# Moving the 28th row of a weight tile onto eight DMA engines in a decode kernel, with two rows added on VectorE

## The chip, the cores and the metric

The kernel runs on one core of one Trainium2 chip. The metric is device time in microseconds (us), measured over repeated executions. "Span" is the time from the first to the last recorded instruction of the core; the difference "time minus span" is what a run costs around that.

The profile names the engines PE (TensorE matmul), PEld (its weight load), DVE (VectorE), ACT (ScalarE), POOL (GpSimd) and SP (SyncE, which here only issues loads). The core has 16 DMA engines, which this document numbers 0 to 15.

## The reference, cut to what matters

One token: attention over a long cache, plus a small MLP, summed into one row of 1,024 numbers.

```python
x = A_x                                  # [1, 1, 1024] bf16
xn = _layernorm(x, axis=-1)
return x + _A_ref(xn, k_cache, v_cache, wq, wo) + _B_ref(xn, w1, w2, w3, w4)

# _A_ref: q = x @ wq (32 heads of 128); softmax(q k^T / sqrt(128)) v over 65,536 keys
#         and 4 kv heads; then @ wo
# _B_ref: ... gelu(layernorm(x1) @ w3) @ w4 ...      w4 is [3584, 1024]
```

Weights and caches are 169.87 MB of bf16 and each byte is used once, so the kernel is a stream of loads with arithmetic hidden under it.

## The kernel before

The loads go one after another through one queue into three slots of 8 MB. The last two are V of the last unit and w4. In w4's slot each of the 128 partitions holds 28 rows of 1,024 numbers (2 KB each); they come in pieces of 8, 12, 5, 2 and 1 rows per partition, so that TensorE can work on a piece while the next ones arrive. The code calls row c of all partitions together column c of w4.

```python
W4_PIECES = (8, 12, 5, 2, 1)
FIRST = 3;  AT_ONCE = 1;  NARROW = 8;  AHEAD = 5
...
elif it == "w4":
    w4_v = B_w4.rearrange("(m c) n -> m c n", c=FC)          # FC = 28
    c0 = 0
    for n in W4_PIECES:
        go(out=t[:, c0 * D:(c0 + n) * D], in_=w4_v[:, c0:c0 + n, :].rearrange("p c n -> p (c n)"))
        c0 += n
```

Everything is summed in one PSUM tile psB (two halves of 512). The x row enters by two float32 matmuls early, the wo rows of three head groups by two float32 matmuls at 384 us. The tail (the last NARROW = 8 of the 28 columns of w4) goes by matmuls of 256 columns to two other PSUM tiles, which four float32 matmuls join with psB:

```python
copy_projection()                    # wo rows of three groups: PSUM -> SBUF
summed = compute_v(NU - 1)
with tc.issue_after(summed):
    add_projection()                 # 2 float32 matmuls into psB
compute_w4(0, FIRST)                 # columns 0..2 of w4
with tc.issue_after(tail["gathered"]):       # "gathered": the matmul pm_e of the last group
    compute_w4(FIRST, early)         # columns 3..7
projected = project(HKV - 1)
with tc.issue_after(projected):
    compute_w4(early, FC - NARROW)   # columns 8..19: the 12-row piece, 24 matmuls
nc.scalar.copy(out=sums[:], in_=psB[0:64, :])
...
narrow_rows(FC - NARROW, FC - NARROW + AHEAD, start=True)     # the 5-row piece, 20 matmuls
quarter_acc(lambda j: ident_f[...], lambda j, h: sums[:, 256 * h:256 * (h + 1)])   # psB joins
narrow_rows(FC - NARROW + AHEAD, FC)                          # the 2- and 1-row pieces, 12 matmuls
nc.scalar.copy(out=out_t[:, 0, :], in_=quarters[0][0:64, 0:256])
nc.vector.tensor_copy(out=out_t[:, 1, :], in_=quarters[1][64:128, 0:256])   # the last cast
nc.scalar.dma_start(out=..., in_=out_t[31:33]...)
```

## Time and profile before

| | before |
|---|---|
| time, median of 3 (range) | 400.86 us (400.77 to 400.88) |
| profiled run: time, span, mean granted clock | 400.66, 398.7, 0.812 |
| last landing of the 12-row piece | 391.50 us |
| last landing of w4 (one-row piece) | 396.50 us |
| start of the last VectorE cast | 396.90 us |

The page of the kernel before, parts 2 and 3: the busy tenths of the DMA engines in 40 slices of the span, then each queue with its packets, megabytes and share of the 16 engines' time.

```profile
DMA  9998999999999999999999999999999998999996
q1 hardware_dynamic: 4128, 169.87, 98.9%
q8 instruction: 9, 0.15, 0.2%
q14 instruction: 1, 0.01, 0.0%
```

The load queue keeps the engines busy for 98.9% of the span, so nothing under it is worth anything by itself. Queue 8 moves nine blocks of instructions.

The chain of waits of the kernel before, its end (start us, us, what):

```profile
363.39 33.10 DMA big<-in_B_w_dram
396.50 0.04 issue
396.54 0.34 PE pm_r L504 x4
396.88 0.02 issue
396.90 0.43 DVE out_t L521
```

The run ends with w4's loads; only four matmuls and a cast stand between the last landing and the store.

The timeline of PE in the kernel before, from 384 us (start us, us, engine, line, operation, operands, count, and in brackets the idle time before it and its releaser):

```profile
385.02 0.82 PE L225 MATMUL psB<-big,hT 128*32 128x512 bf16 x6
386.76 0.49 PE L438 MATMUL pm_e<-ol,sel8big 128*128 128x129 f32 x2 [0.92 <-DVE ol L437]
387.18 1.25 PE L225 MATMUL psB<-big,hT 128*32 128x512 bf16 x10
388.33 1.90 PE L225 MATMUL psB<-big,oT 128*32 128x512 bf16 x16
391.54 2.77 PE L225 MATMUL psB<-big,hT 128*32 128x512 bf16 x24 [1.31 <-DMA big<-in_B_w_dram]
...
396.54 0.29 PE L504 MATMUL pm_r<-big,hT 128*32 128x256 bf16 x4 [0.24 <-DMA big<-in_B_w_dram]
```

TensorE waits 1.31 us for the 12-row piece and again 0.24 us for the last row: it has some slack at each piece. The last four matmuls start 0.04 us after the last landing, and the cast 0.40 us after it.

Each DMA engine adds one to a load's semaphore when its share has landed, and the trace records the time of each increment. This is the one-row piece of the kernel before, sorted (the trace doesn't say which engine is which):

```
394.61 394.62 394.65 394.76 394.84 394.94 394.98 | 395.76 | 396.08 396.23 396.28 396.30 396.31 396.33 396.45 396.50
```

Seven engines are done 1.5 to 1.9 us before the last eight, and one stands between. Early in the run all 16 are within 0.46 us. After each 16 KB block of instructions (queue 8, about 1.05 us each) one more engine stands about 1.5 us further back; after the one block of 8 KB (queue 14, 0.33 us, at 113.21) one engine goes from at most 0.42 to 1.19 us back. Eight of the nine 16 KB blocks are through by 384.1 us, and eight engines form the late group.

### The profile page before, as it was taken

How to read it: one execution, taken by the hardware profiler on the slowest of the kernel's cores; microseconds unless marked ns; L12 is line 12 of the kernel's file. 1: busy time of each engine (PE TensorE's matmuls, PEld its weight loads, DVE VectorE, ACT ScalarE, POOL GpSimd, SP SyncE). 2: the span in 40 equal slices, each digit the busy share in tenths (PEclk: the TensorE clock that was granted, in tenths of full speed). 3: DMA queues.
4: the chain of work that ended last, by engine and by line, in shares of the span. 5: the costliest groups of instructions: out<-in, count | busy, mean ns of one | idle time of the engine just before them, and what ended most of it. 6: DMA issues, size and time to landing. Idle time of an engine off the chain costs nothing.

```text
span 398.7 us, 2595 instructions
## 1 busy us (share of the span) xinstructions
PE 229.6 (58%) x1372; PEld 44.2 (11%) x878; DVE 209.4 (53%) x155; ACT 27.6 (7%) x36; POOL 5.3 (1%) x28
## 2 busy tenths in 40 slices
PE   0461960591569238733974296519462955394996
PEld 0210000010100010011001010200020101010132
DVE  0620010974296559633963795269439942894140
ACT  1001010003000200020002000200110001002000
POOL 2000000000000000000000000000000000000000
PEclk9995996596869787966695889679956896698799
DMA  9998999999999999999999999999999998999996
GB/s 421 421 443 377 444 434 487 441 421 421 416 422 434 421 480 442 421 421 427 422 434 427 447 460 427 416 427 427 441 429 427 454 441 385 418 460 429 409 432 254
DMA packets 4144, 170.03 MB, mean 427 GB/s; under 512 B 419, under 2 KB 421, under 8 KB 678
## 3 DMA queue, kind: packets, MB, share of 16 engines
q1 hardware_dynamic: 4128, 169.87, 98.9%
q8 instruction: 9, 0.15, 0.2%
q14 instruction: 1, 0.01, 0.0%
q10 hardware_dynamic: 6, 0.00, 0.0%
HBM read 169.87 MB, written 0.00 MB: 426 GB/s over the span
## 4 chain that ended last, share of the span: by engine, by line
DMA 56%; DVE 21%; PE 17%; ACT 2%; another core or an unknown queue 2%; issue 1%; SPq 0%; DVEq 0%; ACTq 0%
DMA big<-in_A_k_cache_dram 42%; DVE big L361 15%; PE sc L366 11%; DMA big<-in_B_w_dram 8%; DMA big<-in_A_wq_dram 5%; PE oacc L416 4%; DVE p_sb L387 2%; DVE mx L371 2%; ACT p_sb L384 2%; PE psq L291 1%; SPq L187 0%; PE pm_mx L373 0%; DVE m L375 0%; PE pm_mx L380 0%
## 5 line engine op out<-in xcount | busy, mean ns | idle before, releaser
L366 PE MATMUL sc<-big,qdiag 128*128 128x512 bf16 x512 | 129.3, 414 | 67.0 <-DVE big L361 61.4
L361 DVE STREAM_TRANSPOSE big<-big 128x4096 f32<-128x4096 f32 x32 | 139.4, 4413 | 50.3 <-DMA big<-in_A_k_cache_dram 50.3
L416 PE MATMUL oacc<-big,p_sb 128*32 128x512 bf16 x512 | 43.0, 502 | 34.5 <-DVE p_sb L387 34.5
L371 DVE TENSOR_REDUCE mx<-sc 128x1 f32<-128x2048 f32 x8 | 18.3, 2292 | 29.8 <-PE sc L366 29.8
L366 PEld LDWEIGHTS <-qdiag 128*128 128x128 bf16 x128 | 13.2, 103 | 178.7 <-issue 145.9
L384 ACT ACTIVATE p_sb<-sc,nball 128x2048 bf16<-128x2048 f32 x8 | 15.7, 1967 | 220.9 <-DVE nball L382 220.9
L387 DVE STREAM_TRANSPOSE p_sb<-p_sb 128x2048 bf16<-128x2048 bf16 x8 | 18.5, 2311 | 18.0 <-ACT p_sb L384 18.0
L416 PEld LDWEIGHTS <-p_sb 128*32 128x32 bf16 x512 | 16.1, 122 | 58.2 <-DVE p_sb L387 35.1
L291 PE MATMUL psh<-big,ln_rep_b 128*32 128x512 bf16 (+1 forms) x64 | 12.4, 943 | 8.8 <-DMA big<-in_B_w_dram 8.8
L456 PE MATMUL o_acc<-big,oT 128*1 128x512 bf16 x48 | 13.2, 445 | 2.4 <-ACT p_sb L384 2.4
L373 PE MATMUL pm_mx<-ident_f,mx 128*1 128x128 f32 x8 | 2.4, 296 | 19.1 <-DVE mx L371 19.1
L425 DVE SCALAR_TENSOR_TENSOR og<-oacc,wb,og 128x512 f32<-128x512 f32 x4 | 3.0, 751 | 18.4 <-PE oacc L416 18.4
L330 DVE STREAM_TRANSPOSE h_row<-h_row 128x896 bf16<-128x896 bf16 x1 | 1.1, 1111 | 22.0 <-ACT h_row L329 22.0
L239 PE MATMUL pm_ln<-ln_rowsum_a,ones_f 128*128 128x1 f32 x2 | 0.6, 348 | 12.8 <-DVE ln_rowsum_a L237 12.8
L438 PE MATMUL pm_e<-ol,sel8big 128*128 128x129 f32 x8 | 2.3, 370 | 8.8 <-DVE ol L437 8.8
L315 POOL COPY qdiag<-qx 32x32 bf16<-32x32 bf16 x16 | 3.2, 202 | 279.3 <-PE sc L366 250.9
L230 DVE STREAM_TRANSPOSE x_t<-x_row 32x256 bf16<-32x256 bf16 x4 | 2.5, 616 | 8.3 <-DMA x_row<-in_A_x_dram 8.3
L463 DVE COPY big<-o_acc 1x1024 f32<-1x1024 f32 x1 | 1.2, 1211 | 10.5 <-PE o_acc L456 10.5
L225 PE MATMUL psB<-big,hT 128*32 128x512 bf16 x40 | 4.8, 380 | 1.3 <-DMA big<-in_B_w_dram 1.3
L291 PE MATMUL psq<-big,ln_rep_a 128*32 128x512 bf16 x64 | 5.0, 482 | 0.9 <-DMA big<-in_A_wq_dram 0.9
L521 DVE CAST out_t<-pm_r 64x256 bf16<-64x256 f32 x1 | 0.4, 426 | 8.6 <-PE pm_r L504 8.6
L380 PE MATMUL pm_mx<-ident_f,rep 1*128 1x1 f32 x8 | 1.8, 229 | 5.0 <-DVE rep L377 5.0
(101 smaller groups left out, 76.2 us busy)
## 6 DMA issues: line engine op xcount, KB each, us to landing
big<-in_A_wo_dram SPq DMA_DIRECT2D x1, 8192.0 KB, 35.8
big<-in_B_w_dram SPq DMA_DIRECT2D x1, 7168.0 KB, 38.0
big<-in_B_w_dram SPq DMA_DIRECT2D x3, 2048.0 KB, 35.5
big<-in_B_w_dram SPq DMA_DIRECT2D x1, 3072.0 KB, 29.5
big<-in_B_w_dram SPq DMA_DIRECT2D x1, 1280.0 KB, 32.2
big<-in_B_w_dram SPq DMA_DIRECT2D x1, 512.0 KB
big<-in_B_w_dram SPq DMA_DIRECT2D x1, 256.0 KB, 33.1
big<-in_A_k_cache_dram SPq DMA_DIRECT2D x8, 42.3
```

Of the source, the lines that this page charges most:

```text
L225: return nc.tensor.matmul(psB[32 * j:32 * j + 32, :], lhsT=lhsT.to_broadcast([lhsT.shape[0], 32]), rhs=rhs, start=start, stop=False, tile_ ...
L230: nc.vector.transpose(out=x_t[32 * a:32 * a + 32].rearrange("p c j -> p (c j)"), in_=x_row[:, 256 * a:256 * (a + 1)].rearrange("p (i c) -> ...
L291: nc.tensor.matmul(acc[32 * q:32 * q + 32, i, 0:n], lhsT=rep[:, c, :], rhs=cols(c, i, q), start=(c == 0), stop=(c == DC - 1), tile_positio ...
L315: nc.gpsimd.tensor_copy(out=qdiag[at, LEAD:].rearrange("p (x c) -> p x c", x=4)[:, :, 32 * a:32 * a + 8], in_=qx[at, :, 8 * g:8 * g + 8])
L361: nc.vector.transpose(out=words, in_=words)
L366: nc.tensor.matmul(sc[:, e, :], lhsT=qdiag[:, c0:c0 + P], rhs=cols[:, s, e, :, b2, :, r], start=(s == 0 and b2 == 0 and r == 0), stop=(s = ...
L371: nc.vector.reduce_max(out=mx[:], in_=sc[:].rearrange("p e n -> p (e n)"), axis=AX.X)
L384: nc.scalar.activation(out=p_sb[:], in_=sc[:], func=ACTF.Exp, bias=nball[:, b:b + 1], scale=SCALE, accum_out=group["lall"][:, b:b + 1])
L387: nc.vector.transpose(out=flat, in_=flat)
L416: mm = nc.tensor.matmul(oacc[32 * q:32 * (q + 1), :], lhsT=pT[:, e, 32 * t:32 * (t + 1)], rhs=vt[:, :, e, t, :], start=(e == 0 and t < 4), ...
L425: nc.vector.scalar_tensor_tensor(out=og[:], in0=oacc[:], scalar=wb[:, 1:2], in1=og[:], op0=ALU.mult, op1=ALU.add)
L456: nc.tensor.matmul(tail["rows"][0:1, h2, :], lhsT=oT[g][:, j:j + 1], rhs=wt[:, g, j, 512 * h2:512 * (h2 + 1)], start=(g == 0 and j == 0), ...
```

## The change

Intent: give the early engines more of w4 and the late ones less. Each partition loads 27 rows, not 28. The 128 rows that are left (one per partition, 256 KB) go in six small loads to every fourth of 5 or 8 partitions, which are meant to be written by engines 0 to 7. A row then lies in another partition than its h value, so the slot's extra area is zeroed by GpSimd, and four small matmuls with a 0/1 matrix place the h values. To make room, the x row and the wo rows are no longer summed by float32 matmuls but added on VectorE.

```diff
-W4_PIECES = (8, 12, 5, 2, 1)
+W4_PIECES = (8, 12, 4, 2, 1)
+LEFT = 4
+SHARES = ((5, 0, 4), (5, 1, 4), (5, 2, 4), (5, 3, 4), (8, 32, 4), (8, 33, 2))   # partitions, first, rows each
+WHOLE = 27
-NARROW = 8
-AHEAD = 5
+NARROW = 7
+AHEAD = 4
...
+                nc.gpsimd.memset(t[:, WHOLE * D:(WHOLE + LEFT + 1) * D].bitcast(F32), 0.0)
+                for share in SHARES[:3] + W4_PIECES[:1] + SHARES[3:] + W4_PIECES[1:]:
+                    if share in W4_PIECES:
+                        ...                                   # as before
+                    k, i0, m = share
+                    go(out=t[i0:i0 + 4 * k:4, WHOLE * D:(WHOLE + m) * D].rearrange("e (i n) -> e i n", i=m),
+                       in_=w4_v[m0:m0 + k * m, WHOLE, :].rearrange("(i e) n -> e i n", e=k))
...
-    for j in range(2):
-        row_acc(j, ident_f[0:1, 0:1], accx[0:1, ...], start=True)          # x by matmul
+        nc.vector.tensor_copy(out=x_halves[32 * j:32 * j + 1, :], in_=x_row[0:1, 512 * j:512 * (j + 1)])
+    place = ...                                               # 0/1 matrix, GpSimd
+        nc.vector.tensor_copy(out=h_left[:], in_=h_row[:, 32 * WHOLE:32 * WHOLE + 1])
+    def place_left(): ...                                     # 4 matmuls, one VectorE copy into hT[:, 27:31]
...
     def copy_projection():
-        nc.vector.tensor_copy(out=tail["o"]..., in_=tail["rows"][0:1, 0:2, :])
+        nc.vector.tensor_scalar(out=tail["o"][0:64, :], in0=x_halves[:], ...)
         for j in range(2):
-            row_acc(j, ident_f[0:1, 0:1], tail["o"][:, 512 * j:512 * (j + 1)])
+            nc.vector.tensor_tensor(out=row, in0=tail["rows"][0:1, j, :], in1=row, op=ALU.add)
...
+        compute_w4(WHOLE, WHOLE + LEFT)                       # 8 matmuls over the left rows
-        compute_w4(early, FC - NARROW)
+        compute_w4(early, WHOLE - NARROW)
-    nc.scalar.copy(out=sums[:], in_=psB[0:64, :])
+    nc.vector.tensor_tensor(out=sums[:], in0=psB[0:64, :], in1=tail["o"][0:64, :], op=ALU.add)
...
-    quarter_acc(ident_f ..., sums ...)                        # 4 float32 matmuls
+    pick = ...                                                # a VectorE copy
+    for h in range(2): nc.tensor.matmul(...)                  # 2 float32 matmuls
```

Engines 0 to 4 would so carry 22 of the left rows each, 5 to 7 six, 8 to 15 none, where each carried eight before.

More of the change, by code (lines that the diff above doesn't have):

```diff
@@ L126 @@
     assert DH == P and HQ // HKV == 8 and HKV == 4 and D == 1024 and F == 3584 and S == 1
-    assert SK % UKEYS == 0 and sum(W4_PIECES) == FC
+    assert SK % UKEYS == 0 and sum(W4_PIECES) == WHOLE == FC - 1
     NB = SK // UKEYS
@@ L184, in load @@
                 w4_v = B_w4.rearrange("(m c) n -> m c n", c=FC)
-                c0 = 0
-                for n in W4_PIECES:
-                    go(out=t[:, c0 * D:(c0 + n) * D], in_=w4_v[:, c0:c0 + n, :].rearrange("p c n -> p (c n)"))
-                    c0 += n
+                nc.gpsimd.memset(t[:, WHOLE * D:(WHOLE + LEFT + 1) * D].bitcast(F32), 0.0)
+                c0, m0 = 0, 0
+                for share in SHARES[:3] + W4_PIECES[:1] + SHARES[3:] + W4_PIECES[1:]:
+                    if share in W4_PIECES:
+                        go(out=t[:, c0 * D:(c0 + share) * D], in_=w4_v[:, c0:c0 + share, :].rearrange("p c n -> p (c n)"))
+                        c0 += share
+                        continue
+                    k, i0, m = share
+                    go(out=t[i0:i0 + 4 * k:4, WHOLE * D:(WHOLE + m) * D].rearrange("e (i n) -> e i n", i=m),
+                       in_=w4_v[m0:m0 + k * m, WHOLE, :].rearrange("(i e) n -> e i n", e=k))
+                    m0 += k * m
+                assert m0 == P and c0 == WHOLE
             else:
@@ L215 @@
             in_=ident_f[:, 64 * b:64 * b + 64].rearrange("p (i r) -> p r i", r=2).unsqueeze(2).to_broadcast([P, 2, 4, 32]))
+    x_halves = const.tile([64, 512], BF16, name="x_halves")
+    nc.gpsimd.memset(x_halves[:], 0.0)
     qdiag = const.tile([P, LEAD + 4 * P], BF16, name="qdiag")
@@ L280 @@
     nc.vector.tensor_tensor(out=ln_s2[:], in0=negmean1[:], in1=rstd1[:], op=ALU.mult)
-    accx = ppool.tile([1, D], F32, name="accx", tag="p")
-    nc.vector.tensor_scalar(out=accx[:], in0=x_row[0:1, :], scalar1=ln_s1[0:1, 0:1], scalar2=ln_s2[0:1, 0:1],
-                            op0=ALU.mult, op1=ALU.add)
     for j in range(2):
-        row_acc(j, ident_f[0:1, 0:1], accx[0:1, 512 * j:512 * (j + 1)], start=True)
+        nc.vector.tensor_copy(out=x_halves[32 * j:32 * j + 1, :], in_=x_row[0:1, 512 * j:512 * (j + 1)])
+    place = ogpool.tile([P, LEFT, P], BF16, name="place", tag="og")
+    nc.gpsimd.memset(place[:], 0.0)
+    m0 = 0
+    for k, i0, m in SHARES:
+        cells = place[:, 0:m, i0:i0 + 4 * k:4].rearrange("p i e -> p e i")
+        nc.gpsimd.affine_select(out=cells, in_=cells, compare_op=ALU.not_equal, fill=1.0, base=-m0,
+                                pattern=[[-1, k], [-k, m]], channel_multiplier=1)
+        m0 += k * m
     def row_matmul(acc, rep, cols, widths):
@@ L317, in place_queries @@
                 in_=qx[at, :, 8 * g:8 * g + 8])
-    hT = const.tile([P, FC], BF16, name="hT")
+    hT = const.tile([P, WHOLE + LEFT], BF16, name="hT")
+    h_left = const.tile([P, 1], BF16, name="h_left")
     def compute_w3():
@@ L330, in compute_w3, with place_left @@
         nc.vector.transpose(out=h_row[:], in_=h_row[:])
-        nc.vector.tensor_copy(out=hT[:], in_=h_row[:, ::32])
+        nc.vector.tensor_copy(out=hT[:, 0:WHOLE], in_=h_row[:, 0:32 * WHOLE:32])
+        nc.vector.tensor_copy(out=h_left[:], in_=h_row[:, 32 * WHOLE:32 * WHOLE + 1])
+    def place_left():
+        pm = ps_M.tile([P, 512], F32, name="pm_h", tag="pm")
+        for x in range(LEFT):
+            nc.tensor.matmul(pm[:, x:x + 1], lhsT=place[:, x, :], rhs=h_left[:],
+                             start=True, stop=True)
+        nc.vector.tensor_copy(out=hT[:, WHOLE:], in_=pm[:, 0:LEFT])
     def compute_w12():
@@ L343, in compute_w12 @@
             for j in range(2):
-                row_acc(j, g_col[:], wt[:, 1, c, 512 * j:512 * (j + 1)])
+                row_acc(j, g_col[:], wt[:, 1, c, 512 * j:512 * (j + 1)], start=(c == 0))
         st.done("w12")
@@ L461, in copy_projection @@
     def copy_projection():
-        tail["o"] = st.tiles["w4"][0:1, FC * D:FC * D + 2 * D].bitcast(F32)
-        nc.vector.tensor_copy(out=tail["o"].rearrange("p (j n) -> p j n", j=2), in_=tail["rows"][0:1, 0:2, :])
-    def add_projection():
+        tail["o"] = st.tiles["w4"][:, (WHOLE + LEFT) * D:(WHOLE + LEFT + 1) * D].bitcast(F32)
+        nc.vector.tensor_scalar(out=tail["o"][0:64, :], in0=x_halves[:], scalar1=ln_s1[0:64, 0:1], scalar2=ln_s2[0:64, 0:1],
+                                op0=ALU.mult, op1=ALU.add)
         for j in range(2):
-            row_acc(j, ident_f[0:1, 0:1], tail["o"][:, 512 * j:512 * (j + 1)])
+            row = tail["o"][32 * j:32 * j + 1, :]
+            nc.vector.tensor_tensor(out=row, in0=tail["rows"][0:1, j, :], in1=row, op=ALU.add)
     def compute_w4(lo, hi):
@@ L477 @@
     compute_w12()
+    place_left()
     for u in range(NU - 1):
@@ L485 @@
     copy_projection()
-    summed = compute_v(NU - 1)
-    with tc.issue_after(summed):
-        add_projection()
+    compute_v(NU - 1)
     early = sum(W4_PIECES[:AT_ONCE])
@@ L512, in narrow_rows @@
                         start=start and c == lo)
-    narrow_rows(FC - NARROW, FC - NARROW + AHEAD, start=True)
-    quarter_acc(lambda j: ident_f[0:64, 32 * j:32 * j + 1].to_broadcast([64, 32]),
-                lambda j, h: sums[:, 256 * h:256 * (h + 1)])
-    narrow_rows(FC - NARROW + AHEAD, FC)
+    narrow_rows(WHOLE - NARROW, WHOLE - NARROW + AHEAD, start=True)
+    pick = small.tile([64, 2, 32], F32, name="pick", tag="msk")
+    nc.vector.tensor_copy(out=pick[:],
+                          in_=ident_f[0:64, 0:64].rearrange("p (j r) -> p j r", r=32)[:, :, 0:1].to_broadcast([64, 2, 32]))
+    for h in range(2):
+        nc.tensor.matmul(quarters[h][64 * h:64 * h + 64, 0:256], lhsT=pick[:].rearrange("p j r -> p (j r)"), rhs=sums[:, 256 * h:256 * (h + 1)], start=False,
+                         stop=False, tile_position=(0, 64 * h), skip_group_check=True)
+    narrow_rows(WHOLE - NARROW + AHEAD, WHOLE)
     out_t = ogpool.tile([64, 2, 256], BF16, name="out_t", tag="og")
```

## The prediction

> **What bounds the kernel.** The page's DMA row shows the 16 engines at 9 tenths or more in nearly every slice; queue 1 takes 98.9% of their span and moves 169.87 MB. The chain of waits ends with 33.10 us of w4 loads (363.39 to 396.50), then four matmuls (0.34 us), the last cast (0.43) and the store. So only two things can shorten the run: the moment at which the last w4 piece has landed, and the 2.2 us behind it.
>
> **What the change aims at.** The trace's semaphore increments give each engine's landing. Early on (wq) the 16 spread over 0.46 us. For each 16 KB instruction fetch (queue 8, about 1.05 us, some 256 PE instructions apart) one engine drops back by about 1.5 us. At the end two groups stand: the last one-row piece lands on 7 engines at 394.61 to 394.99, on one at 395.76, on eight at 396.09 to 396.50. Mean 395.6: perfect balance could give at most about 0.9 us.
>
> The Trainium skill ("DMA: Bandwidth & Descriptors", The descriptor swizzle) says that partitions 0 to 63 are served by engines 0 to 7, four neighbours each (and +32); the same page (Why a DMA increments its semaphore by 16) says that a load with outer dimension k runs on the lowest k engines. So engines 0 to 4 would take 4·4+4+2 = 22 rows of 2 KB, 5 to 7 six, 8 to 15 none, instead of 8 each. The trace has no engine numbers; that the late ones are 8 to 15 I infer from the change.
>
> **Cost.** Single 2 KB packets take 84 ns, 10 KB 387; four rows instead of five save each engine 0.62 us.
> - Engines 8 to 15: 396.50 - 0.62 = 395.9.
> - Engines 0 to 4: 394.6..395.0 - 0.62 + 22·0.084 + six completions (about 0.1) = 395.95..396.35.
> Last landing about 396.2, 0.3 earlier. Engines 0 to 4 become the last.
>
> The 12-row piece lands at about 391.8 instead of 391.5 (extra rows in front).
>
> **PE tail.** 24 matmuls (2.77 us) end at about 394.6 instead of 394.3. The addition on VectorE (0.7 us, from the 0.69 of a 128x512 addition) replaces ScalarE's 0.58, hidden behind 16 narrow matmuls. Two float32 matmuls replace four (0.64 us). PE reaches the last row at about 396.1, near the landing; last matmul at about 396.6 instead of 396.88. The eight matmuls of the left rows fit PE's 1.31 us idle before the 12-row piece.
>
> **Off the path.** POOL's memset of 128x2560 (estimate 2 to 3 us from 0.54 for 536) waits for the slot (361.6) and the first share for it, but V7's load occupies DMA until 377. In the compiled order the 12-row piece waits on V7's semaphore (379.3), the next three on shares: issued about 379.4 to 381, before the first engine runs dry at about 382.3. This wait is new; slack 1 to 2 us. The x matmuls of the first 20 us (wq lands at 21.9) and the four float32 matmuls at 384 cost nothing either way.
>
> **Prediction.** 400.5 us, 8 in 10 within 400.15 to 400.9; faster by 2% 0.01, same 0.98, slower 0.01.
>
> **Right if** the last piece's landings spread over under 0.8 us instead of 1.9 and end at 396.0 to 396.4, and cast and store stay. **Wrong if** one of engines 0 to 4 is a late one (the end moves to 397, 0.5 lost), if small loads cost more than 84 ns a row, if the 12-row piece's issue leaves engines dry, or if PE is late at 396.

## The result, and the profile after

Ratios are the mean time of one kernel's fast runs over that of the other's of the same rounds, so not quite the ratio of the medians quoted.

| | before | after |
|---|---|---|
| time, median (range, runs) | 400.88 us (400.77 to 401.12, 6) | 401.61 us (401.37 to 403.05, 6) |
| ratio after / before | | 1.0026 [1.001, 1.0041] |
| span, median of the runs | 398.7 (profiled run) | 399.15 |
| time minus span | 1.96 (profiled run) | 2.35 to 2.49, median 2.47 |
| last landing of the 12-row piece | 391.50 | 392.37 |
| last landing of w4 | 396.50 | 396.78 |
| start of the last VectorE cast | 396.90 | 397.36 |

The change costs 0.73 us (0.18%) where 0.36 us of gain was predicted. By the medians the span grew by about 0.45 us and the time outside it by about as much (2.47 against 2.03, the median of 58 later runs of the kernel before). That the two make more than 0.73 is scatter between calls.

The same parts of the page of the kernel after:

```profile
DMA  9998999999999999999999999999999999999895
q1 hardware_dynamic: 4292, 169.87, 98.8%
q8 instruction: 9, 0.15, 0.1%
```

The stream is as dense as before: nothing was lost by dry queues.

The chain of waits of the kernel after, its end:

```profile
386.50 0.80 PE pm_e L465 x2
387.30 7.90 PE psB L238 x31
...
395.46 0.69 DVE sums L524
...
396.20 0.65 PE pm_r L546 x4
396.85 0.50 PE pm_r L531 x12
...
397.36 0.43 DVE out_t L552
```

In this profile no load stands at the end any more. TensorE works without a pause from 386.50 to 395.4, then VectorE's addition, the float32 matmuls and the last twelve narrow ones follow.

The timeline of PE in the kernel after:

```profile
386.50 0.80 PE L465 MATMUL pm_e<-ol,sel8big 128*128 128x129 f32 x2 [2.65 <-DVE ol L464]
387.23 3.01 PE L238 MATMUL psB<-big,hT 128*32 128x512 bf16 x16
390.07 1.89 PE L238 MATMUL psB<-big,oT 128*32 128x512 bf16 x16
391.80 3.40 PE L238 MATMUL psB<-big,hT 128*32 128x512 bf16 x30
```

TensorE was idle for 2.65 us in front of pm_e (0.92 before), and the 16 matmuls after it took 3.01 us where ten took 1.25. The table of stretches of the kernel after shows why (columns: stretch, its length, then busy share and count of PE, PEld, DVE, ACT, POOL, then the granted clock, the DMA share and GB/s):

```profile
386.00:387.00 1.00, 0.50 (x2) 0.50 (x2) 0.44 (x1) 0.00 (x0) 0.00 (x0) 0.54 0.92 393
387.00:388.00 1.00, 1.00 (x6) 0.28 (x6) 0.67 (x3) 0.00 (x0) 0.00 (x0) 0.50 0.97 418
388.00:389.00 1.00, 1.00 (x8) 0.39 (x6) 0.93 (x5) 0.00 (x0) 0.00 (x0) 0.50 1.03 442
```

The clock was granted at a half for 3.41 us: the trace's own clock records have it from 386.09 to 389.50. The Trainium skill ("TensorE: Matmul & The Clock Gate", Why this matters for your kernels) advises against idle gaps of more than about 3 us; here 2.65 us were enough in this run.

The landings of the two pieces that matter, after:

```
12-row piece: 389.63 390.04 390.05 | 391.12 391.23 391.28 391.42 391.42 391.43 391.44 391.45 391.49 391.51 391.64 391.75 | 392.37
one-row piece: 394.04 394.44 394.45 | 395.49 395.61 395.65 395.77 395.78 395.79 395.80 395.82 395.86 395.89 396.03 396.13 | 396.78
first share (5 engines, 4 rows each): 377.72 377.75 377.80 377.83 378.69
```

One engine is 0.6 us behind all others at the end, and of the five engines of the first share one is 0.9 us behind already. Most engines did land 0.5 us or so earlier than the late ones of before, as intended.

So three theories were on the table:

- **E** (TensorE): the idle time before pm_e, with the three columns and the half clock behind it, makes TensorE late at the end.
- **D** (DMA): one of engines 0 to 4 (it turned out to be 3) is a late one and is given 22 rows. In its later form: the 12-row piece can't be used until engine 3 has brought it, and from there TensorE and VectorE need about 4.8 us to the last cast, so that landing, and not the last row's, sets the end. (The traces bear out the load on engine 3, but not this last distinction; see the section on again and again2.)
- **V** (VectorE): the changed kernel has a longer stream of VectorE instructions, and that sets the time outside the span.

### The profile page after: what moved, and what is told of

Read it like the earlier page. It is cut to its first block, busy times and chain, and to the rows that moved or that the text cites. A ratio compares the mean times of both kernels' runs of the same rounds, so it can differ in the third digit from the quotient of the medians.

```text
span 399.1 us, 2625 instructions
## 1 busy us (share of the span) xinstructions
PE 231.0 (58%) x1368; PEld 45.7 (11%) x874; DVE 211.4 (53%) x162; ACT 27.1 (7%) x35; POOL 9.8 (2%) x37
## 3 DMA queue, kind: packets, MB, share of 16 engines
q1 hardware_dynamic: 4292, 169.87, 98.8%
## 4 chain that ended last, share of the span: by engine, by line
DMA 54%; PE 26%; DVE 17%; ACT 2%; issue 1%; DVEq 0%; ACTq 0%
DMA big<-in_A_k_cache_dram 44%; DVE big L388 11%; PE sc L393 10%; DMA big<-in_B_w_dram 10%; PE oacc L443 5%; PE o_acc L483 3%; PE psh L309 3%; PE psB L238 2%; DVE mx L398 2%; ACT p_sb L411 2%; DVE p_sb L414 2%; PE ps L365 1%; DVE m L402 0%; PE pm_mx L400 0%; DVE ol L464 0%
## 5 line engine op out<-in xcount | busy, mean ns | idle before, releaser
L393 PE MATMUL sc<-big,qdiag 128*128 128x512 bf16 x512 | 130.7, 418 | 63.6 <-DVE big L388 58.1
L443 PE MATMUL oacc<-big,p_sb 128*32 128x512 bf16 x512 | 44.8, 519 | 34.5 <-DVE p_sb L414 34.5
L309 PE MATMUL psq<-big,ln_rep_a 128*32 128x512 bf16 x64 | 6.4, 590 | 4.1 <-DMA big<-in_A_wq_dram 4.1
L238 PE MATMUL psB<-big,hT 128*32 128x512 bf16 x48 | 6.6, 435 | 0.0
L449 ACT COPY og<-oacc 128x512 f32<-128x512 f32 x4 | 2.3, 587 | 33.9 <-PE oacc L443 25.5
```

The lines of the kernel that those rows point to most:

```text
L238: return nc.tensor.matmul(psB[32 * j:32 * j + 32, :], lhsT=lhsT.to_broadcast([lhsT.shape[0], 32]), rhs=rhs, start=start, stop=False, tile_ ...
L309: nc.tensor.matmul(acc[32 * q:32 * q + 32, i, 0:n], lhsT=rep[:, c, :], rhs=cols(c, i, q), start=(c == 0), stop=(c == DC - 1), tile_positio ...
L393: nc.tensor.matmul(sc[:, e, :], lhsT=qdiag[:, c0:c0 + P], rhs=cols[:, s, e, :, b2, :, r], start=(s == 0 and b2 == 0 and r == 0), stop=(s = ...
L443: mm = nc.tensor.matmul(oacc[32 * q:32 * (q + 1), :], lhsT=pT[:, e, 32 * t:32 * (t + 1)], rhs=vt[:, :, e, t, :], start=(e == 0 and t < 4), ...
```

## The experiments

Eighteen runs were made, two of them of the changed kernel unedited, each timed against the kernel before on the same chip (the two maps: one look). Diffs are against the kernel after unless said otherwise. "Cast" is the start of the last VectorE cast in the profiled run; "gap" is time minus span.

| run | time | span | gap | kernel before, same call | ratio [95%] | 12-row piece | last landing | cast |
|---|---|---|---|---|---|---|---|---|
| warm | 401.39 | 398.9 | 2.53 | 400.80 | 1.0018 [1.0005, 1.003] | 393.01 | 397.37 | 397.78 |
| d_only | 401.21 | 399.1 | 2.15 | 400.80 | 1.0014 [1.0, 1.0027] | 392.24 | 396.62 | 397.02 |
| a_only | 400.92 | 398.7 | 2.24 | 400.80 | 1.0 [0.9988, 1.0013] | 391.49 | 396.47 | 396.88 |
| again | 401.43 | 398.95 | 2.47 | 400.77 | 1.0011 [0.9997, 1.0025] | 392.40 | 396.76 | 397.17 |
| shares3 | 401.70 | 399.15 | 2.55 | 400.77 | 1.0013 [0.9999, 1.0028] | 392.51 | 396.90 | 397.30 |
| a_late | 401.15 | 398.8 | 2.21 | 400.77 | 1.001 [0.9988, 1.0033] | 392.04 | 397.02 | 397.43 |
| again2 | 401.92 | 399.3 | 2.62 | 400.69 | 1.0033 [1.002, 1.0047] | 392.63 | 397.00 | 397.41 |
| spare3 | 401.22 | 398.6 | 2.54 | 400.69 | 1.0022 [1.0009, 1.0034] | 392.04 | 396.41 | 396.82 |
| heavy3 | 402.23 | 399.7 | 2.53 | 400.69 | 1.004 [1.0028, 1.0053] | 392.88 | 397.24 | 397.65 |
| half | 400.82 | 398.3 | 2.58 | 400.77 | 0.9997 [0.9983, 1.001] | 391.44 | 396.11 | 396.49 |
| moved | 401.24 | 399.2 | 2.00 | 400.82 | 1.0011 [0.9998, 1.0024] | 392.58 | 396.95 | 397.48 |
| half_moved | 400.32 | 398.2 | 2.11 | 400.82 | 0.9989 [0.9976, 1.0001] | 391.60 | 396.22 | 396.60 |
| moved_six | 401.71 | 399.3 | 2.35 | 400.94 | 1.002 [1.0007, 1.0033] | 392.71 | 397.07 | 397.56 |
| six_dve | 401.46 | 399.4 | 2.05 | 400.82 | 1.0012 [0.9998, 1.0026] | | | |
| six_pool | 400.64 | 398.6 | 2.12 | 400.82 | 0.9997 [0.9984, 1.0009] | | | |
| twelve_dve | 400.68 | 398.6 | 2.05 | 400.94 | 0.9996 [0.9983, 1.0009] | | | |

Times, spans and gaps are medians. The kernel before had a gap of 1.95 to 2.14 in all its 58 runs of these calls.

### warm: the early w4 columns back in front of the gathering matmul

```diff
-FIRST = 3
+FIRST = 7
@@ compute_v, last group
+            with tc.issue_after(mm.ins):
+                tail["first"] = compute_w4(0, FIRST)
@@ group_rows
+        with (tc.issue_after(tail["first"]) if g == HKV - 1 else nullcontext()):
             tail["gathered"] = nc.tensor.matmul(pe[:, 0:DH + 1], ...)
```

> The changed kernel with seven w4 columns issued on TensorE before the gathering matmul instead of after it, so TensorE does not sit idle for 2.65 us at 383.85 and its granted clock should stay 1.0 from 386 to 389. Theory E (TensorE late): the loss comes from the half clock; time 400.5 to 400.9. Theory D (one late DMA engine among 0 to 4 that got 22 extra rows): the last landing stays at 396.8 and the 12-row piece at 392.4, so the time stays above before, 401.1 to 401.4.

Measured: 401.39 us, span 398.9 against 399.15. The profiled run kept the full clock, so the edit did what it should. It was this kernel's slowest run (402.13) and engine 3 stood 1.66 us back in it, so its landings are late, beyond what D had expected (396.8 and 392.4). By the median spans, E is worth 0.25 us or less; the loss mostly stays, and the time lies in D's range and not in E's.

### d_only and a_only: each half of the change alone

d_only keeps the shares and puts the x and wo rows back on TensorE; a_only is the kernel before with the additions on VectorE.

```diff
@@ d_only, against after
-    nc.vector.tensor_tensor(out=sums[:], in0=psB[0:64, :], in1=tail["o"][0:64, :], op=ALU.add)
+    nc.scalar.copy(out=sums[:], in_=psB[0:64, :])
+    # accx, add_projection and the four picking matmuls as in the kernel before
@@ a_only, against before
-    row_acc(j, ident_f[0:1, 0:1], ...)          # x and wo rows by matmul
+    nc.vector.tensor_tensor(out=row, in0=tail["rows"][0:1, j, :], in1=row, op=ALU.add)
+    # x_halves, pick and the addition into sums as in the kernel after
```

> The load split alone: x and wo rows and the final sums as before on TensorE and ScalarE. Theory E: TensorE stays busy around 384 with the float32 matmuls, clock 1.0, time 400.5 to 400.9. Theory D: one engine's last landing at 396.8 against 396.5, 12-row piece at 392.4 against 391.5, time 401.1 to 401.5.

> The additions on VectorE alone, loads as before (8, 12, 5, 2, 1). The compiled order keeps three w4 columns before the gathering matmul. Theory E in its wide form (the missing float32 matmuls let the clock fall): clock 0.5 somewhere in 384 to 390 and time 401.2 to 401.6. Theory D: landings as before (396.5), time 400.8 to 401.0.

Measured: d_only 401.21 us with span 399.1, which is the span of the whole change; a_only 400.92 us with span 398.7, that of the kernel before. The chain of waits of d_only, its end:

```profile
379.24 13.00 DMA big<-in_B_w_dram
...
392.28 2.78 PE psB L236 x24
...
397.02 0.42 DVE out_t L554
```

With a full clock, and an idle time before pm_e of 1.66 us in place of 2.65 (the columns still stand behind pm_e), the 12-row piece lands at 392.24 and the cast starts 4.78 us later. The chain doesn't show that the last four matmuls here waited for the last row: it landed at 396.62, they start at 396.66, 0.26 us after the four before them, and where nothing is waited for (the changed kernel's first profile) these groups follow at 0.11 us. The loss in the span belongs to the loads alone: D holds, E falls for the largest part. In gap, neither half has all of it (2.15 and 2.24 against 2.47): it needs both.

### map1 and map2: which engines are late

The kernel before, with six more loads over the first k partitions behind the 12-row piece. The Trainium skill ("DMA: Bandwidth & Descriptors", Why a DMA increments its semaphore by 16 and not by 1) says that a load with an outer size of k up to 16 runs on the lowest k engines. So where two loads differ by one in k, the landing that the larger has more is engine k - 1's.

```diff
@@ against before (map1; map2: 14, 13, 12, 11, 10, 9)
+                    if n == 12:
+                        for i, k in enumerate((7, 6, 5, 4, 3, 2)):
+                            at = 30 * D + 256 * i
+                            go(out=t[0:k, at:at + 256], in_=B_w4[0:k, 0:256])
```

> The kernel before with six small extra loads of 512 bytes a partition, over 7, 6, 5, 4, 3 and 2 partitions, queued behind the 12-row piece: as each runs on the lowest so many engines, the landing that is missing from one to the next is that of engine 6, 5, 4, 3 and 2. Theory D: exactly one of engines 0 to 4 lands 0.8 us or more behind the others. Theory E: none of engines 0 to 4 does. The time means nothing here.

> As map1 with loads over 14, 13, 12, 11, 10 and 9 partitions: names engines 13 to 9. If the late ones are engines 8 to 15, as the change supposes, all of 9 to 13 land 1.5 us behind; by map1's count (five early and three late among 0 to 7, eight early in all at that time or seven) two of engines 8 to 15 are early. The time means nothing here.

Measured in map1:

```
k=7: 389.69 389.77 389.90 390.20 391.05 391.35 391.68
k=6: 389.87 389.97 390.09 390.39 391.24 391.88
k=5: 390.05 390.16 390.26 390.57 391.42
k=4: 390.23 390.46 390.77 391.62
k=3: 390.42 390.64 391.03
k=2: 390.81 391.21
```

Each load shows exactly k landings, and each is the row above without one, about 0.19 us later, as the skill says. From k=7 to k=6 the one at 391.35 is missing: engine 6 is late. From 6 to 5, 391.68's: engine 5 is late. From 5 to 4, 389.77's: 4 is early. From 4 to 3, 391.05's: engine 3 is late, by about an us. 0, 1 and 2 are early. map2 shows the same way that 9 to 13 are late by 1.6 to 2.0 us, 7 and 8 early, and one of 14 and 15 early, the other late. (One look each: 401.63 and 401.18 us.)

So the premise "0 to 7 ahead, 8 to 15 behind" is wrong for 3, 5, 6 and 8. Engine 3 is the one of the five that gets 22 rows and is late. Its lateness, about 1 us, fits the 8 KB block, as the one engine that stood between the groups before; that it is the same engine is read from the size only.

### again and again2: the changed kernel, unedited

> The changed kernel once more, unedited, for a second profile and the spread of its times beside the variants of this call. Theory D (engine 3 is a late one and carries 22 rows): one landing of the last row stands alone 0.6 us or more behind the other 15, at 396.7 to 397.4, and times spread more than those of before (401.2 to 402.5), since how late engine 3 is differs from run to run. Theory E: granted clock 0.5 around 386 to 389 again.

> The changed kernel once more, unedited, as the control for the next two on the same chip. By theory D in its present form (the 12-row piece cannot be used before engine 3 has brought it, and TensorE needs 4.7 us from there to its last matmul): 12-row piece at 392.2 to 392.5, time 401.3 to 401.6.

Measured: 401.43 and 401.92 us, on two chips: by medians the loss is 0.7 and 1.2 us (the interval of the first just includes none). Again2's time and 12-row piece (392.63) lie above what had been expected. In again the same 2.65 us of idle time did not lower the clock, against what E had expected. The stretches of again:

```profile
386.00:387.00 1.00, 0.94 (x8) 0.59 (x10) 0.42 (x4) 0.00 (x0) 0.00 (x0) 1.00 0.92 393
387.00:388.00 1.00, 1.00 (x14) 0.42 (x11) 0.96 (x4) 0.00 (x0) 0.00 (x0) 1.00 1.03 442
```

And its chain of waits, the end:

```profile
379.26 13.14 DMA big<-in_B_w_dram
...
392.44 2.78 PE psB L238 x24
...
395.24 0.69 DVE sums L524
...
395.98 0.65 PE pm_r L546 x4
396.63 0.52 PE pm_r L531 x12
...
397.17 0.43 DVE out_t L552
```

With the full clock TensorE catches up and waits for the 12-row piece; the cast starts 4.77 us after it, in again2 4.78. In the first profile of the changed kernel, with the half clock, it was 4.99, because TensorE was through with psB only at 395.44 (395.22 in again). So the half clock cost about 0.2 us in that run, and without it the chain shows the load.

The chain leads to the 12-row piece, but the last row is as near. The trace holds the start of each matmul; the last twelve are three groups of four, and the third group needs the last row:

| | second group starts | third group starts | between | last row landed | cast after that landing |
|---|---|---|---|---|---|
| before | 396.00 | 396.54 | 0.54 | 396.50 | 0.40 |
| after | 396.89 | 397.00 | 0.11 | 396.78 | 0.58 |
| again | 396.68 | 396.81 | 0.13 | 396.76 | 0.41 |
| again2 | 396.91 | 397.04 | 0.13 | 397.00 | 0.41 |
| d_only | 396.40 | 396.66 | 0.26 | 396.62 | 0.40 |
| spare3 | 396.32 | 396.45 | 0.13 | 396.41 | 0.41 |
| heavy3 | 397.16 | 397.29 | 0.13 | 397.24 | 0.41 |

In "after" nothing is waited for, and the groups follow at 0.11 us. In again, again2, spare3 and heavy3 the third group starts 0.04 to 0.05 us after the last landing, as before the change, so the path over the 12-row piece and the path over the last row end within about 0.02 us of each other. Both pieces are late by the same engine, and no run holds one of them back alone: which of the two sets the end is not shown.

### shares3: fewer rows on engine 3, part of the rows loaded over all 16 engines

```diff
-SHARES = ((5, 0, 4), (5, 1, 4), (5, 2, 4), (5, 3, 4), (8, 32, 4), (8, 33, 2))
+SHARES = ((5, 0, 4, 4), (3, 1, 4, 4), (3, 2, 4, 4), (3, 33, 4, 4), (8, 32, 1, 4), (16, 3, 4, 8))   # + partition step
```

> The changed kernel with other shares only: engine 3 spared. Engines 0, 1 and 2 take 21 of the rows, 3 and 4 nine, 5 to 7 five, 8 to 15 four. Estimate from the landings of before: engines 0 to 2 end at 396.2, engine 3 at 396.0, 5 and 6 at 396.3, 8 to 15 at 396.3. Theory D: last landing 396.2 to 396.4, 12-row piece at 391.9 instead of 392.4, time 0.3 to 0.6 us below the changed kernel of the same call. Theory E (TensorE's clock alone): no gain over the changed kernel within 0.15 us.

Measured: 401.70 us, and a miss for D as it was then put. The 11 latest landings of the last piece lay at 396.59 to 396.90, where I had expected 396.2 to 396.4. What differs from all the other versions is one load over 16 engines that writes every eighth partition, so that 14 of the 16, by the map of partitions that the prediction takes from the skill, write partitions that another engine serves. The trace shows where the time went: between 382 and 385 us 23 of the 128 packets of 24 KB took over 1.0 us (914 ns is the median; in again and in spare3 one packet does so), and all packets from 377.3 us on took 18.1 us per engine in place of 17.3. That the odd load slows its neighbours would explain this, but it was not measured alone, so this run can't be counted for or against engine 3.

### a_late: the additions alone, with the columns behind the gathering matmul

```diff
@@ against a_only
-    compute_w4(0, FIRST)
     with tc.issue_after(tail["gathered"]):
-        compute_w4(FIRST, early)
+        compute_w4(0, early)
```

> The additions alone, with loads as before, and all eight first w4 columns issued behind the gathering matmul, as the changed kernel's compiled order has it: TensorE then waits about 2.5 us after the last V matmul. Theory E: clock 0.5 from about 386 to 389, 32 matmuls at 0.21 us, TensorE reaches the 12-row piece at about 392 and not 391.5, time 0.2 to 0.5 us above the additions alone (400.92). Theory D: landings as before, time within 0.15 us of it.

Measured: 401.15 us, wide (400.77 to 403.20), span 398.8 against 398.7 of a_only. The time is 0.23 us above a_only's 400.92, which is in E's range and not in D's; but a_only ran on another chip, and the interval against the kernel before (0.9988 to 1.0033) decides nothing. The idle time is there and the profiled run's clock fell to a half, and still the median span hardly moves; an early 12-row piece leaves TensorE slack before it, which would explain that. The profiled run had an engine 2.6 us late and says nothing of the rest. By the median span E alone makes no loss of this size; by the time this run leaves it open. (Two of its six runs had gaps of 2.88 and 3.40, the others 2.17 to 2.24.)

### spare3 and heavy3: no big share for engine 3, or a bigger one

```diff
-SHARES = ((5, 0, 4), (5, 1, 4), (5, 2, 4), (5, 3, 4), (8, 32, 4), (8, 33, 2))
+SHARES = ((3, 0, 4), (3, 1, 4), (3, 2, 4), (3, 3, 4), (8, 32, 4), (8, 33, 4), (8, 34, 2))            # spare3: engine 3 has 10 rows
+SHARES = ((4, 0, 4), (4, 1, 4), (4, 2, 4), (4, 3, 4), (4, 32, 4), (4, 33, 4), (8, 34, 4))            # heavy3: engine 3 has 28 rows
```

> Only the shares differ from the changed kernel[...]: engines 0 to 2 take 26 rows, 3 to 7 take 10, so engine 3 loses 12 rows. Theory D: engine 3 no longer lands alone; the late engines 5 and 6 with two or four more rows than in the changed kernel and the loaded 0 to 2 set the end: 12-row piece at 391.9 to 392.2, last landing 396.4 to 396.7, time 0.15 to 0.4 us below the changed kernel of this call, still above before. Theory E (TensorE alone): no difference within 0.1.

> As spare3 with seven loads, but engines 0 to 3 take 28 rows and 4 to 7 take four: engine 3 gets six more rows than in the changed kernel (6 x 0.084 = 0.5 us). Theory D: engine 3 alone last by over 1 us, 12-row piece at 392.8 to 393.0, last landing 397.2 to 397.4, time 0.35 to 0.6 us above the changed kernel of this call. Theory E: no difference within 0.1; a mere count of loads: the same as spare3.

Measured beside again2, on the same chip: spans 398.6 (10 rows), 399.3 (22 rows), 399.7 us (28 rows). The chain of waits of spare3, its end:

```profile
380.05 12.00 DMA big<-in_B_w_dram
...
392.08 2.78 PE psB L238 x24
...
396.82 0.43 DVE out_t L552
```

And of heavy3:

```profile
380.09 12.79 DMA big<-in_B_w_dram
...
392.92 2.78 PE psB L238 x24
...
397.65 0.43 DVE out_t L552
```

The cast follows the 12-row piece by 4.78 and 4.77 us in the two, and the last row by 0.41 in both. Rows on engine 3 move both pieces, and the end moves with them: this shows D in its plain form. The first shares name engine 3 in these kernels too: one engine stands 0.74 us behind the others in heavy3's load over four engines (378.68), none in spare3's over three. From 22 to 28 rows six times 84 ns, 0.5 us, were due: the spans say 0.4, the profiled pieces 0.25. Times are less exact than the landings: spare3 lies 0.70 us below again2 (0.15 to 0.4 expected) and heavy3 0.31 above it (0.35 to 0.6 expected). spare3's span is that of the kernel before and its time is still 0.5 us worse: its gap is 2.54.

### half: only half of each row moves

With 3, 5 and 6 late, five of engines 0 to 7 are early. An estimate from the numbers above: taking a whole row off everyone brings 0.62 us; 128 rows of 84 ns over five engines add 2.15 us to engines that stood at 394.6 to 395.0. They would end at 396.1 to 396.5, no better than 396.50. Half of that, 1.08 us, is what the gap between the groups can take. So the first halves stay (a 1 KB piece per partition) and only the second halves go, mostly to engines 0, 1, 2. This version also has warm's order.

```diff
-W4_PIECES = (8, 12, 4, 2, 1)
-LEFT = 4
-SHARES = ((5, 0, 4), (5, 1, 4), (5, 2, 4), (5, 3, 4), (8, 32, 4), (8, 33, 2))
+W4_PIECES = (8, 12, 5, 2)
+LEFT = 6
+SHARES = ((3, 0, 6), (3, 1, 6), (3, 2, 6), (3, 3, 6), (5, 32, 6), (8, 33, 3), (2, 34, 1))
-                       in_=w4_v[m0:m0 + k * m, WHOLE, :].rearrange("(i e) n -> e i n", e=k))
+                       in_=w4_v[m0:m0 + k * m, FC - 1, 512:].rearrange("(i e) n -> e i n", e=k))
+                go(out=t[:, c0 * D:c0 * D + 512], in_=w4_v[:, c0, 0:512])
```

> Made from what the map of engines says, on the additions-alone kernel: only the second half (1 KB) of each 28th row moves, 33 or 34 half rows to each of engines 0 to 2, nine to 3, six or more to 4, three to 5 to 7, none to 8 to 15; the first halves go as one load over 128 partitions; the seven first w4 columns stay ahead of the gathering matmul. Theory D, by an estimate of 0.045 us per half row: engines 8 to 15 land at 396.2, 0 to 2 at 396.1 to 396.3, 12-row piece at 391.5 to 391.7, time 0.1 to 0.35 us below before. If a 1 KB piece costs much more than half of 2 KB, engines 0 to 2 end after 396.5 and nothing is gained.

Measured: last landing 396.11, span 398.3, which is 0.4 us better than the kernel before. The time is 400.82, equal to it, because the gap is 2.58.

### six_dve, six_pool, twelve_dve: nothing but more instructions

Against the kernel before, six or twelve tiny memsets on VectorE, or six on GpSimd:

```diff
+    spare = const.tile([P, 8], F32, name="spare")
+    for i in range(6):
+        nc.vector.memset(spare[:, i:i + 1], 0.0)        # six_pool: nc.gpsimd; twelve_dve: range(12)
```

> The kernel before with six memsets of one element a partition added on VectorE in its idle time near 16 us. Theory V (the length of VectorE's instruction stream sets the time outside the span, by a fetch at its end): time minus span 2.4 to 2.6 instead of 2.0, span unchanged at 398.7, time 401.15 to 401.3. Otherwise: 2.0, time 400.8.

> The same six memsets on GpSimd. Theory V: time minus span 2.0, time 400.8. If the length of GpSimd's stream does it (it is longer in the changed kernel too): 2.4 to 2.6 and 401.2.

> The kernel before with twelve idle memsets on VectorE: 185 recorded instructions, as in the changed kernel. If the count alone matters, with a threshold between 180 and 185: time minus span 2.4 to 2.6, span 398.7, time 401.1 to 401.3. If it is the work and not the count: 2.0 to 2.15 and 400.8.

Measured: gaps of 2.05, 2.12 and 2.05 us. Six more instructions do nothing to the gap. Of the five runs with twelve, two had a gap of 2.51 and 2.58, and three 1.98 to 2.05; the kernel before never had one over 2.14. (six_dve's time is 401.46 because three of its spans were 399.4 to 399.6; its gap is what it was run for. Why those spans were long is open.)

### moved, half_moved, moved_six: VectorE's copies elsewhere

```diff
@@ moved, against after (half_moved: the same against half)
-        nc.vector.tensor_copy(out=x_halves[...], in_=x_row[...])      # two of these
+        nc.scalar.copy(out=x_halves[...], in_=x_row[...])
-        nc.vector.tensor_copy(out=h_left[:], ...)
+        nc.scalar.copy(out=h_left[:], ...)
-        nc.vector.tensor_copy(out=hT[:, WHOLE:], in_=pm[:, 0:LEFT])
+        nc.scalar.copy(out=hT[:, WHOLE:], in_=pm[:, 0:LEFT])
-    nc.vector.tensor_copy(out=pick[:], ...
+    nc.gpsimd.tensor_copy(out=pick[:], ...
@@ moved_six, on top of moved
+    for i in range(6):
+        nc.vector.memset(spare[:, i:i + 1], 0.0)
```

> The changed kernel with four or five of its new small copies (x halves, the left column, its four placed columns) on ScalarE and one (the picking matrix) on GpSimd, so VectorE has 131 rows instead of 136. Theory V: time minus span 2.0 to 2.2 instead of 2.5, span as before the move (398.9 to 399.3), time 401.0 to 401.2, no 8 KB fetches after the end. Otherwise: 2.5 and 401.4 to 401.9.

> The same move on the variant with half rows (span 398.2 to 398.3). Theory V: time minus span 2.0 to 2.2, time 400.3 to 400.5, that is 0.3 to 0.5 us below before. Otherwise 400.8 as before.

> The changed kernel with its small copies moved off VectorE (2.0 us outside the span) and six idle memsets put on VectorE instead: 186 recorded instructions. If the count alone matters: 2.4 to 2.6 again, time 401.4 to 401.7. If it is the work: 2.0 and 401.0 to 401.3.

Measured: the gap falls from 2.47 (after) to 2.00, and from 2.58 (half) to 2.11, with the spans unchanged. (TensorE starts on the float32 matmuls 0.14 us after VectorE's addition in moved and moved_six, elsewhere 0.04. The picking copy itself can't be what it waits for: GpSimd is through with it at 388.34 in moved. Why is open.) Six memsets on top of moved bring it to 2.33, 2.37, 2.54 and 2.86 in four of six runs, and leave it at 2.0 in two. The working VectorE instructions of the page, beside the gap:

| | before | moved, half_moved | d_only | a_only | six_dve | after, again, half | moved_six | twelve_dve |
|---|---|---|---|---|---|---|---|---|
| VectorE instructions | 155 | 157 | 158 | 160 | 161 | 162 | 163 | 167 |
| gap, median | 2.0 | 2.00, 2.11 | 2.15 | 2.24 | 2.05 | 2.47, 2.47, 2.58 | 2.35 | 2.05 |

The gap answers to VectorE's stream: taking five instructions off it removes 0.47 us, twice (the gap of the kernel before was 1.95 to 2.14 in all 58 of its runs), and putting useless ones on brings it back in some runs. But it is no simple count: 167 instructions gave the long gap in only two runs of five, and 162 in nearly all. What else in the stream decides is open.

The fetch that theory V names was not confirmed. The traces go on past the span, and queue 14 there has blocks of 8 KB of instructions, 1.8 to 2.3 us after its end: two in every profiled execution with a gap of 2.37 us or more (nine of them), none in those of before, a_only, d_only, a_late and the three with memsets (1.96 to 2.24). But moved has one with a gap of 2.04, and half_moved two with 2.11, where "no 8 KB fetches after the end" had been expected of moved. So these fetches go with the long gap and don't by themselves make it.

half_moved is the best version: 400.32 us (400.21 to 400.51) against 400.82 on the same chip. Its ratio of 0.9989 has an interval up to 1.0001, so the gain of 0.1% is as large as what five rounds can tell apart. The chain of waits of half_moved, its end:

```profile
380.53 14.16 DMA big<-in_B_w_dram
...
394.74 0.73 PE pm_r L537 x20
395.46 0.58 PE pm_r L552 x4
396.04 0.53 PE pm_r L537 x10
...
396.60 0.42 DVE out_t L558
```

The chain leads to the 5-row piece (landed at 394.69), and the 12-row piece, at 391.60, is off it. But the last two matmuls start at 396.26, 0.04 us after the last landing (396.22) and 0.17 us after the group before them (0.11 where nothing is waited for), so here the last piece sets the end, by about 0.06 us. The cast is 0.30 us earlier than before.

## Why the prediction was wrong

- **"engines 0 to 4 take 22 rows, 5 to 7 six, 8 to 15 none"**: right as far as the traces show it. Five-partition loads showed five landings, as the skill's rule has it ("DMA: Bandwidth & Descriptors", Why a DMA increments its semaphore by 16 and not by 1), and four rows took 0.32 to 0.35 us, so about 84 ns a row as costed. The 395.9 given for the late engines without left rows fits too: twelve landings, these six among them by the maps, lie at 395.49 to 396.13.
- **"that the late ones are 8 to 15 I infer from the change"**: this step failed. The maps show 3, 5, 6, 9 to 13 and one of 14 and 15 late, and 8 early. Engine 3 was late by about 0.9 us and got 22 rows. The same sum with the right start has it: 395.76 (the engine between the groups) - 0.62 + 22·0.084 + 0.1 = 397.1; measured 396.78, against "396.2". The text named this case under "Wrong if", with the end at 397 and 0.5 us lost, but gave it too little weight for its range. Reading the engine numbers off the change's own intent was taking the claim under test as evidence for it.
- **"The 12-row piece lands at about 391.8"**: it landed at 392.37, by the same engine. From there TensorE's tail ran as costed (24 matmuls 2.78 us, addition 0.69, float32 0.65, narrow ones 0.52: 4.8 us with the issue). But it ran behind a piece 0.6 us later than thought. In the first profile, with the half clock, it became the end (the last four matmuls start 0.22 us after the last row's landing). In again, again2, spare3 and heavy3 it ends within 0.02 us of what the last row allows, so the two late pieces can't be told apart there.
- **"cast and store stay"**: this step failed too. It took the end of the span for the end of the run. The time outside the span grew by about 0.45 us; moved and half_moved show that it goes when five copies are taken off VectorE, and how these copies make it stays open.
- **"PE's 1.31 us idle" holds the eight new matmuls**: they went in, but three columns had moved behind pm_e as well and TensorE stood idle for 2.65 us. With the half clock TensorE was through with psB at 395.44 in the changed kernel's first profile and at 395.46 in moved; that costs what it exceeds the 12-row piece's landing and 2.82 us by, 0.2 us in the first and under 0.1 in the second. Not foreseen; the compiled order showed the move.
- **Off the path**: right. The memset took 2.23 us from 361.63, no engine ran dry, and queue 1's share was 98.8%.
- **The spread "under 0.8 us"**: it was 2.7 us (394.04 to 396.78).

Put together: the predicted cast was at about 396.6. The last row came 0.58 us later and the 12-row piece 0.57, and the half clock added 0.2, which gives the 397.36 that was measured; 0.45 us outside the span makes up most of the rest of the 1.1 us between 400.5 and 401.61.

Four things stay open: what beside its length in VectorE's stream sets the time outside the span, whether the 12-row piece or the last row sets the end at full clock, why the packets were slow in shares3, and why some executions of the changed kernels scatter more (in their profiles engine 3 landed 0.87 to 1.66 us behind the first engine of its first share). That the last explains the slower of the unprofiled runs was only argued.

## What to carry to other kernels

Before moving bytes between DMA engines, measure which of them are late: a few nested loads over 2 to 7 partitions at the place in question cost one run and tell it by engine number. A rebalancing must start each engine's sum from where that engine stands, must not move more than the lag holds, and should count the landing of every piece that a later stage needs: here the loaded engine brought the 12-row piece late as well, which took away TensorE's slack. And watch time minus span beside the span: small copies put on an engine far from the critical path changed it here by as much as the whole gain sought.

## What the Trainium skill lacked or had wrong

- "DMA: Bandwidth & Descriptors", Latency and other measured facts, has engines 7 and 15 as usually slower than the others, and as particular to loads issued by GpSimd. Here, with loads issued by SyncE, engine 7 was early, which agrees with that limit. What the page lacks is that other engines can lag in such loads: 3, 5, 6, 9 to 13 and one of 14 and 15 were late by 0.9 to 2.0 us.
- "Runtime: NRT & Kernel Launch", Instruction fetch mechanics, calls the cost of a fetch "mostly hidden". The block size agrees (nine transfers of 16,384 bytes). But each puts one DMA engine about 1.5 us back, and one of 8,192 bytes about 0.8, which a kernel bound by loads sees at its end: landings spread over 1.9 us there, against 0.46 us at the start.
- "TensorE: Matmul & The Clock Gate", Why this matters for your kernels, gives about 3 us as the idle gap to stay under. Here a gap of 2.65 us halved the clock in three profiles (the changed kernel's first, moved, a_late) and not in six others with the same gap (again, again2, shares3, spare3, heavy3, moved_six). The free-running window of Part 1 of that page fits this: in all 20 kept traces the clock records change only on a grid of 3.413 us, whose place in the span differs from one to the next. In the three profiles a step of the grid came after 2.24, 2.28 and 2.44 us of the idle time, in the six after 1.26 to 1.98. So a gap shorter than 3 us can be enough, by where the grid falls.
- No page says that the time outside the span changes with an engine's instruction stream: 2.47 us against 2.00 with five copies moved off VectorE, 2.58 against 2.11 in the second pair.
- No page gives what a load costs whose engines write partitions that other engines serve: with one such load over 16 engines (shares3), 11 engines landed at 396.59 to 396.90 where 396.2 to 396.4 was expected, and packets took 18.1 us per engine in place of 17.3. It was not measured alone.
